# DeltaNet attention followed by a SwiGLU feed-forward block on one core: turning K and x with transfers and VectorE instead of TensorE

## The chip, the cores and the metric

The kernel runs on one core of a Trainium2 chip. The metric is the device time of one execution in microseconds (us), lower is better. A core has five engines with a queue of instructions each: TensorE (PE in the profile; its weight loads are the row PEld), VectorE (DVE), ScalarE (ACT), GpSimd (POOL) and SyncE (SP, which here only issues transfers). Sixteen DMA engines move the data of the transfers.

## The reference

There are 4 batches of 8 heads, 768 steps and a head dimension of 48. The result of the attention (`x`, 3072 tokens by 384) goes through a feed-forward block with 1536 inner columns. All is 32-bit floating point.

```python
k_n = k / (np.linalg.norm(k, axis=-1, keepdims=True) + 1e-06)
for t in range(S):
    kt, vt, bt = (k_n[:, :, t], v[:, :, t], beta[:, :, t, None])
    y[:, :, t] = np.einsum('bhd,bhde->bhe', q[:, :, t], state)
    v_old = np.einsum('bhde,bhd->bhe', state, kt)
    state = state + bt[:, :, :, None] * np.einsum('bhd,bhe->bhde', kt, vt - v_old)
x = y.transpose(0, 2, 1, 3).reshape(B * S, H * D)
rms = np.sqrt(np.mean(x * x, axis=-1, keepdims=True) + 1e-06)
xn = x / rms * rms_g
g = xn @ w_gate
out = (g * (1.0 / (1.0 + np.exp(-g))) * (xn @ w_val)) @ w_out
```

## The kernel before

The 768 steps are cut into 12 chunks of 64 steps, numbered c = 0 to 11; a chunk holds all 32 pairs of batch and head. Each chunk passes through these parts.

- `load` brings K, Q and V of the chunk into SBUF, with steps on the partitions. From chunk 2 on, Q comes as 16 small transfers that lay 32x32 squares into the tile `q2`, each square where its turned image belongs; in `qpart` one VectorE instruction (L592) then turns all squares of `q2` in place into `qt`, which has the head dimension on the partitions.
- `norms` and `prep` scale K to unit length (the power on GpSimd at L577, the product on GpSimd at L654), turn it (`turn`, L532 on TensorE into two PSUM banks, L544 on ScalarE out of them into `kt`), multiply it with itself (`scores`, L555), and invert a unit triangular matrix of each pair of batch and head. For the inversion the products go through DRAM (`dkk`) into the tile `at`, GpSimd scales them (L682), VectorE runs fifteen steps of multiply and reduce (L731, L737), and the result goes through DRAM again (`dx`, `dxt`) into `mt`, `x2bd` and `m1bd`; two small merges on TensorE follow (L813, L837).
- `recur` combines the chunk with the state carried from chunk to chunk (L878, L924, L938, L975). The chunk's output stands in `yn`, is normalised there (GpSimd for the root, ScalarE L1040 for the product) and turned on TensorE (L1046, six transposes of 128x128 in two PSUM banks) and scaled by `rms_g` on the way out of PSUM (L1055, six ScalarE instructions) into `xf`, which has the model dimension on the partitions. Seven VectorE sums of columns of `xf` follow (L1070).
- The feed-forward part of chunks 0 and 1 is plain (`ffn_plain`, L1118 and L1100). From chunk 2 on, `ffn` multiplies 3x3 blocks with 15 products instead of 18 for each half of the inner columns (L1211), with factors that VectorE computes once from the weights (`factors`, L1174 and L1176). The partial sums leave PSUM through VectorE (L1221) or ScalarE (L1223), then silu (L1227) and the product (L1228) fill `hf`; `down` makes the output with seven products of 2x2 blocks (L1268) and VectorE sums around them (L1260, L1277).

Single buffers set much of the order: `xf`, `yn`, `q2`, `qt`, `at` and `acc` exist once, `kt` twice, K three times. The next chunk's x can enter `xf` only when the last L1211 product of the chunk before has read it.

The order of instructions is made ahead by a planner in the kernel file (`Plan`). Each step is put in with its engine, an assumed duration, a due time, what it reads and writes, and the PSUM banks it needs. `forward` simulates the queues with those assumed durations, `backward` turns the result into new priorities, 110 rounds are played with small random shakes, and the best order is emitted. The order of each engine's queue is fixed then, and an instruction that waits holds up all that stands behind it on its engine. Transfers are nearly all issued by SP (L407). `turn` is the part of TensorE's work that the change takes away for most chunks:

```python
P.add("PE", 0.44, tr, pr, r=r + ["ident"], w=[ps, keys[hv]], ps=ps, size=8)
```

Of the kernel before, what the change touches and what calls it, by code (L numbers as in the profile page):

```python
# [11 lines left out]
FP32 = mybir.dt.float32  # L12
# [7 lines left out]
W = 32  # L20
# [9 lines left out]
RING, LANES, FIRST, LAND = 2330, 8, 1.08, 0.9  # L30
WARM = 62.0
CLEAR = (0.5, 0.8, 1.1)


class Op:
# [31 lines left out]
class Plan:  # L67
# [47 lines left out]
    def forward(self, banks, until, clear=1.0):  # L115

        at = dict.fromkeys(ENGINES, 0.0)
        held = {"DVE": 0.0, "POOL": 0.0}
        cand = {e: [] for e in ENGINES}
        free = list(banks)  # L120
        for op in self.ops:
            op.wait, op.at = len(op.deps), op.ready
            for g in op.acquire:
                g.taken, g.uses = False, g.left
            if not op.wait:
                cand[op.eng].append(op)
        order, end_, mode = [], 0.0, 0
        server, sent = 0.0, []
        landed = [0.0] * LANES
        soon = sorted((op.past, op.n) for op in self.ops if op.dma and not op.bulk and op.past is not None)  # L130
        backlog = 0.0
        while len(order) < len(self.ops):
            best = None
            for e in ENGINES:
                for op in cand[e]:
                    s = max(op.at, at[e])
                    if op.dma:
                        s = max(s, landed[-LANES])
                        if op.bulk:
                            for t, _ in soon:  # L140
                                if t >= max(server, s + FIRST) + clear * op.work:
                                    break
                                if t > s:
                                    s = t + 0.01
                    if op.port:
                        s = max(s, held["POOL" if e == "DVE" else "DVE"])
                    n = sum(not g.taken for g in op.acquire)
                    if n > len(free):
                        continue
                    if n:  # L150
                        s = max(s, free[n - 1])
                    key = op.key + (STICK if op.mode is not None and op.mode != mode else 0.0)
                    rate, store = (FETCH, AHEAD) if s > EARLY else (FETCH0, AHEAD0)
                    if op.size and backlog + op.size - rate * op.dur > store:
                        key += 2.0 * STICK
                    if best is None or (s, key, op.n) < best[0]:
                        best = ((s, key, op.n), op)
            if best is None:
                return None
            (s, _, _), op = best  # L160
            cand[op.eng].remove(op)
            for g in op.acquire:
                if not g.taken:
                    g.taken = True
                    free.pop(0)
            op.start = s
            if op.mode is not None and op.mode != mode:
                s += 0.1
                op.start, mode = s, op.mode
            end = s + op.dur  # L170
            if op.eng == "PE":
                if s - at["PE"] > 1.4 and s > until:
                    end += 1.6
                rate, store = (FETCH, AHEAD) if s > EARLY else (FETCH0, AHEAD0)
                fill = 6.0 if s < until else 0.0
                backlog = max(0.0, backlog - (rate - fill) * (s - at["PE"])) + op.size - rate * op.dur
                late = max(0.0, backlog - store) / rate
                backlog, end = max(0.0, backlog - rate * late), end + late
            at[op.eng] = end - min(OVERLAP[op.eng], op.dur)
            if op.port:  # L180
                held[op.eng] = end
            end_ = max(end_, end)
            for g in op.release:
                g.uses -= 1
                if not g.uses:
                    free.append(end + 0.1)
                    free.sort()
            if op.dma:
                end = self.room(sent, end, op.desc)
                at[op.eng] = end  # L190
                begun = max(server, s + FIRST)
                server = max(begun + op.work, end)
                if not op.bulk and op.past is not None:
                    soon.remove((op.past, op.n))
                sent.append((begun, server, op.desc))
                end = server + LAND
                landed.append(end)
            op.end = end
            for u in op.users:
                u.wait -= 1  # L200
                u.at = max(u.at, at[op.eng] if u.eng == op.eng and not op.dma else end + op.hop(u) + u.slack)
                if not u.wait:
                    cand[u.eng].append(u)
            order.append(op)
        self.end = end_
        return order
# [78 lines left out]
def kernel(  # L285
# [17 lines left out]
    nc = tc.nc  # L303

    B, H, S, D = q.shape
    NCH = S // C
    DM = H * D
    DFF = moe_w_gate.shape[1]
    KT = DM // 128
# [22 lines left out]
    g_sb = sbt("g_sb", [128, KT])  # L332
# [12 lines left out]
    q2 = sbt("q2", [128, 16, DP])  # L345
# [48 lines left out]
    banks = [psum.tile([128, 512], FP32, name=f"bank{i}") for i in range(8)]  # L394
    dkk = [dram.tile([2, 2, 16, W, W], FP32, name=f"dkk{i}") for i in range(2)]
    dx = [dram.tile([2, 2, 16, W, W], FP32, name=f"dx{i}") for i in range(2)]
    dxt = [dram.tile([W, 2, 16, W], FP32, name=f"dxt{i}") for i in range(2)]

    P = Plan()
# [5 lines left out]
    def dma(dst, src, prio, r=(), w=(), work=0.2, dur=0.53, eng="SP", after=0.0, desc=256, bulk=False):  # L405
        queue = nc.scalar if eng == "ACT" else nc.sync
        op = P.add(eng, dur, lambda: queue.dma_start(out=dst, in_=src), prio, r, w, lat=0.1)  # L407
        op.dma, op.work, op.ready, op.desc, op.bulk = True, work, after, desc, bulk
        op.port = False
# [136 lines left out]
    def scores(kt_, rhs, pr, r, w):  # L546

        ps = [Group(), Group()]

        def sc():  # L550
            for u in range(8):
                for d in range(2):
                    for g in range(2):
                        s, c_ = slice(64 * d, 64 * d + 64), slice(64 * g, 64 * g + 64)
                        nc.tensor.matmul(ps[d].t[c_, 64 * u : 64 * u + 64], kt_[s, u, c_], rhs[s, u, c_])  # L555

        P.rows = 64
        P.add("PE", 0.99, sc, pr, r=r, w=ps + w, ps=ps, size=128)
        P.rows = 128
        return ps  # L560
# [42 lines left out]
    def prep(c):  # L603
# [50 lines left out]
        P.add(n_, 1.6 if c else 1.1, lambda: en.tensor_tensor(  # L654
            out=kd, in0=kd, in1=krec[i2][:, :, None].to_broadcast([128, 16, D]), op=ALU.mult,
        ), pr if early else pn, r=[("krec", i2)], w=kkeys)
        turn(kn, kt[ikq], ktk, kkeys + kp, pr, False)
        ps = scores(kt[ikq], kt[ikq], pr, ktk, kkall)
        for d in range(2):
            dst = kk[ikk][:, :, d:16:2]  # L660
# [195 lines left out]
    def recur(c):  # L856
# [137 lines left out]
        for h in halves:  # L994
# [35 lines left out]
            if c == 0:  # L1030
                for g in range(2):
                    for p in h:
                        P.add("ACT", A(192), lambda p=p, g=g: nc.scalar.activation(
                            out=yn[:, p].rearrange("s (y g e) -> s y g e", g=2, e=D)[:, :, g],
                            in_=psy[g, p].t[:, 192 * p : 192 * p + 192].rearrange("s (y e) -> s y e", e=D),
                            func=ACTF.Copy, scale=rs[i2][:, p : p + 1],
                        ), py, r=[psy[g, p], ("rs", i2, p)], w=[("yn", p)], last=psy[g, p])
            else:
                for p in range(2):
                    P.add("ACT", A(384), lambda p=p: nc.scalar.mul(yn[:, p], yn[:, p], rs[i2][:, p : p + 1]), py, r=[("rs", i2, p)], w=[("yn", p)])  # L1040
            for p in h:
                psx = Group()

# [63 lines left out]
    def ffn_plain(c, f0, f1, start):  # L1107
# [19 lines left out]

        def down(f):
            if f == f0:
                P.add("PE", 0.0, lambda: None, start, r=xk, w=["po"], ps=po[1])  # L1130
            P.add("PE", 1.31, down_mm(po, f, f0, f1), start + 3.9 * (f - f0) + 9, r=[("hf", f, 0), ("hf", f, 1), "wouse"] + ready[("wo", f)], w=["po"], ps=po[0], size=8)

        LAG = 2
# [64 lines left out]
    def ffn(c, start):  # L1198
        n = 0
        for h in range(2):  # L1200
            ps = [Group() for _ in range(3)]
            for m, ((kind, slot), xs, b_, begin, o, more_, end) in enumerate(PRODUCTS):
# [11 lines left out]
                            )  # L1214

                first = ["acq"] if m < 3 else []
                P.add("PE", 0.9, mm, start + 0.95 * n, r=["xc", ("xp", 0), ("xp", 1), ("wx", h)], w=[g] + first, ps=g, size=16)
                n += 1
                t = tmp[:, o]
                if more_:  # L1220
# [108 lines left out]
    for c in range(NCH):  # L1329
# [13 lines left out]
        if c + 1 < NCH:  # L1343
            P.late = c > 0
            load(c + 1, "v")
            P.slack = 0.2
            qpart(c + 1)
            P.late = True
        if c + 2 < NCH:
            load(c + 2, "q")  # L1350
        P.slack, P.lead, P.late = 0.1, 0.0, c > 1
        if c == 1:

# [50 lines left out]
```

## Time and profile before

| | |
|---|---|
| median of 3 runs | 702.61 us (699.99 to 702.84) |
| the profiled execution | 702.7 us, with a span of 700.9 us from first to last instruction |
| granted TensorE clock | 1.000 |
| busy: PE, PEld | 685.0 us, 624.4 us |
| busy: DVE, ACT, POOL | 529.2 us, 311.6 us, 135.4 us |
| transfers | 54.66 MB in 232790 packets |

The profile is of one execution. Busy times are sums over an engine's instructions. Matmuls are pipelined: the duration of one is longer than the distance to the next, so distances between starts in the timeline tell what a group costs. L numbers are lines of the kernel before; 1.8 us of the profiled execution lie outside its span.

### The profile page before, as it was taken

What the parts mean: (1) busy time and instruction counts of PE and PEld (TensorE: products, weight loads), DVE (VectorE), ACT (ScalarE), POOL (GpSimd) and SP (SyncE); (2) the same over time, 40 slices, a digit from 0 to 9 for tenths busy, and PEclk for the clock granted to TensorE, in tenths of its full rate; (3) what the DMA queues carried; (4) which work ended last, traced back from release to release, by engine and by line L of the source; (5) the groups of instructions that cost most, each with busy time, mean ns of one, the idle gap of its engine ahead of it and who ended that gap; (6) DMA issues with size and microseconds to landing.
All of it is one profiled execution on the core that took longest, in us unless ns stands there. A gap on an engine that the chain in (4) does not pass through costs nothing.

```text
span 700.9 us, 23147 instructions
## 1 busy us (share of the span) xinstructions
PE 685.0 (98%) x9930; PEld 624.4 (89%) x9930; DVE 529.2 (76%) x1121; ACT 311.6 (44%) x720; POOL 135.4 (19%) x140
## 2 busy tenths in 40 slices
PE   9999799999999999999999999999999999999997
PEld 5667677787799999999999999999999999999997
DVE  4897794589889679639948969859947968957373
ACT  5256375552244445445344445345345345235241
POOL 6100040111123212132123132122105031000000
PEclk9999999999999999999999999999999999999999
DMA  7875894951623433251073261264153060130101
GB/s 115 154 173 107 196 268 71 273 103 24 119 49 48 82 64 46 43 105 26 21 122 52 39 130 26 40 105 71 35 80 57 13 121 15 24 56 2 23 1 23
DMA packets 232790, 54.66 MB, mean 78 GB/s; under 512 B 221936, under 2 KB 225008, under 8 KB 232688
## 3 DMA queue, kind: packets, MB, share of 16 engines
q1 hardware_dynamic: 227840, 52.27, 39.6%
q10 hardware_dynamic: 4848, 0.92, 0.8%
q8 instruction: 78, 1.28, 0.8%
q14 instruction: 24, 0.20, 0.1%
HBM read 40.83 MB, written 12.32 MB: 76 GB/s over the span
## 4 chain that ended last, share of the span: by engine, by line
PE 73%; DVE 14%; DMA 5%; SPq 3%; POOL 2%; issue 2%; ACT 2%; DVEq 0%; POOLq 0%; ACTq 0%
PE bank L1211 32%; PE bank L1268 18%; PE bank L1118 5%; PE bank L1100 3%; PE bank L555 3%; SPq L407 3%; PE bank L878 2%; PE bank L1368 2%; DMA more<-in_moe_w_gate_dram 2%; DVE tmp L1221 2%; DVE acc L737 2%; DVE acc L731 2%; PE bank L532 2%; PE bank L924 1%; PE bank L837 1%
## 5 line engine op out<-in xcount | busy, mean ns | idle before, releaser
L1211 PE MATMUL bank<-xf,w_in 128*128 128x128 f32 x1440 | 181.0, 277 | 0.0
L1221 DVE TENSOR_TENSOR tmp<-tmp,bank 128x512 f32<-128x512 f32 x180 | 120.9, 683 | 74.6 <-PE bank L1211 57.1
L1211 PEld LDWEIGHTS bank<-xf,w_in 128*128 128x128 f32 x1440 | 170.5, 192 | 3.0 <-issue 1.2
L1211 PE MATMUL bank<-xf,more 128*128 128x128 f32 x960 | 124.6, 277 | 2.1 <-DVE tmp L1221 2.1
L1211 PEld LDWEIGHTS bank<-xf,more 128*128 128x128 f32 x960 | 115.3, 192 | 4.2 <-DVE tmp L1221 3.2
L1223 ACT COPY tmp<-bank 128x512 f32<-128x512 f32 x120 | 68.8, 585 | 92.2 <-PE bank L1211 62.9
L737 DVE TENSOR_REDUCE acc<-acc 128x30 f32<-128x90 f32 (+4 forms) x180 | 85.1, 473 | 6.2
L1227 ACT ACTIVATE tmp<-tmp 128x256 f32<-128x256 f32 x120 | 49.5, 417 | 86.7 <-DVE tmp L1221 86.2
L1268 PE MATMUL bank<-wo_sb,hf 128*128 128x192 f32 x360 | 64.3, 328 | 0.0
L577 POOL TENSOR_TENSOR knrm<-ksum,half 128x16 f32<-128x16 f32 x12 | 36.0, 3003 | 145.7 <-DVE ksum L576 145.7
L731 DVE TENSOR_TENSOR acc<-acc,at 128x60 f32<-128x60 f32 (+4 forms) x165 | 59.1, 358 | 6.6 <-POOL at L714 4.4
L1268 PEld LDWEIGHTS bank<-wo_sb,hf 128*128 128x128 f32 x360 | 58.1, 190 | 0.5
L1228 DVE TENSOR_TENSOR hf<-tmp 128x256 f32<-128x256 f32 x120 | 49.8, 431 | 11.0 <-ACT tmp L1227 10.4
L1368 PE MATMUL bank<-ident 128*128 128x128 f32 (+2 forms) x154 | 45.3, 440 | 1.4 <-POOL ident masks.py:199 1.4
L758 POOL COPY acc<-acc 128x128 f32<-128x128 f32 x40 | 18.1, 480 | 131.9 <-DVE acc L737 131.0
L1368 PEld LDWEIGHTS bank<-ident 128*128 128x128 f32 x154 | 26.2, 197 | 18.4 <-issue 15.7
L1118 PE MATMUL bank<-xf,w_in 128*128 128x256 f32 x144 | 34.9, 386 | 4.1 <-DVE w_in L496 3.7
L682 POOL TENSOR_TENSOR at<-at,beta_b 128x1024 f32<-128x1024 f32 x8 | 18.8, 2356 | 93.4 <-DMA at<-dkk 75.9
L1118 PEld LDWEIGHTS bank<-xf,w_in 128*128 128x128 f32 x144 | 26.4, 190 | 10.4 <-DVE w_in L496 4.5
L1100 PE MATMUL bank<-wo_sb,hf 128*128 128x384 f32 x96 | 33.6, 488 | 0.0
L1118 PE MATMUL bank<-xp,w_in 128*128 128x256 f32 x144 | 33.1, 382 | 0.4 <-DVE hf L1126 0.4
L1118 PEld LDWEIGHTS bank<-xp,w_in 128*128 128x128 f32 x144 | 27.0, 190 | 5.4 <-DVE hf L1126 0.5
(166 smaller groups left out, 980.9 us busy)
## 6 DMA issues: line engine op xcount, KB each, us to landing
at<-dkk SPq DMA_DIRECT2D x21, 256.0 KB, 4.1
vt<-in_v_dram SPq DMA_DIRECT2D x24, 192.0 KB, 4.1
more<-in_moe_w_gate_dram SPq DMA_DIRECT2D x6, 768.0 KB, 7.7
more<-in_moe_w_val_dram SPq DMA_DIRECT2D x6, 768.0 KB, 8.4
more<-in_moe_w_out_dram SPq DMA_DIRECT2D x6, 768.0 KB, 5.8
out_dram<-tmp SPq DMA_DIRECT2D x48, 96.0 KB, 2.3
k<-in_k_dram SPq DMA_DIRECT2D x23, 192.0 KB, 4.1
mt<-dx SPq DMA_DIRECT2D x84, 32.0 KB, 2.0
```

Of the source, the lines that this page charges most:

```text
L577: P.add("POOL", 2.95, lambda: nc.gpsimd.tensor_tensor(out=knrm[i2], in0=ksum[i2], in1=half, op=ALU.pow), pn, r=[("ksum", i2), "half"], w=[ ...
L731: nc.vector.tensor_tensor(out=acc[:, 1:3, 0:n, j + 2 : W].rearrange("p a i t -> p i a t"), in0=acc[:, old, 0:n, j : j + 2, None].to_broadc ...
L737: nc.vector.tensor_reduce(out=acc[:, new, 0:n, j + 2 : W], in_=acc[:, lo : lo + 3, 0:n, j + 2 : W].rearrange("p a i t -> p i t a"), axis=A ...
L1100: nc.tensor.matmul(po[p].t[:, 0:DM], hf[:, spot(f), 128 * p : 128 * p + 128], wo_sb[:, spot(f)], start=(f == f0), stop=(f == f1 - 1), skip ...
L1118: nc.tensor.matmul(ps.t[:, TOK * side : TOK * side + TOK], w_in[:, side, h_, 3 * t + i_, n : n + 128], x_[:, 2 * t : 2 * t + 2].rearrange( ...
L1211: nc.tensor.matmul(g.t[:, 128 * z : 128 * z + 128], fac[:, side, 128 * f : 128 * f + 128], xf[:, xs], start=(begin and z == 0), stop=False ...
L1221: P.add("DVE", V(512), lambda t=t, g=g: nc.vector.tensor_tensor(out=t, in0=t, in1=g.t, op=ALU.add), -1, r=[g], w=[tk], last=g)
L1223: P.add("ACT", A(512), lambda t=t, g=g: nc.scalar.copy(t, g.t), -1, r=[g], w=[tk], last=g)
L1227: P.add("ACT", A(256), lambda t=t: nc.scalar.activation(out=t[:, 0:256], in_=t[:, 0:256], func=ACTF.Silu), -1, w=[tk])
L1228: P.add("DVE", V(256), lambda t=t, f0=f0, p=p: nc.vector.tensor_tensor(out=hf[:, spot(f0) : spot(f0) + 2, 128 * p : 128 * p + 128], in0=t[ ...
L1268: nc.tensor.matmul(g.t[:, 0:192], a_[:, f], b_[:, f], start=(begin and f == 0), stop=(f == 5), skip_group_check=True)
L1368: nc.tensor.matmul(warm[:, 0 : 128 * w_].rearrange("p (w n) -> p w n", n=128), ident, ident[:, None, :].to_broadcast([128, w_, 128]))
```

## The change

For chunks 3 to 11, K is turned in the way that Q already was. After its scaling, sixteen transfers from SBUF to SBUF lay its 32x32 squares into `q2`, which K and Q now use by turns, and one VectorE instruction turns them into `kt`. For chunks 2 to 10, x takes such a way too: four transfers write the normalised `yn` to a DRAM buffer `xd`, four bring it back into `yn` as squares, two VectorE instructions turn it into `xf`, and three ScalarE instructions multiply `xf` by `rms_g` in place. The K of chunks 0 to 2 and the x of chunks 0, 1 and 11 stay on TensorE.

Three smaller edits go with it. The products of K and Q read 48 instead of 64 rows, because the squares leave the rows behind the head dimension unset. The loading of Q is put in ahead of `qpart` of the same chunk, behind the K that shares its buffer. The first three products of each `ffn` wait until the last `ffn_plain` has begun its down products (`begun`). The edits in `forward` skip candidates that can't win and leave its choice the same. The planner works out a new order for the whole kernel.

```diff
+TURNK = range(3, 12)
+TURNX = range(2, 11)
...
+    xd = [dram.tile([4, 128, 6, W], FP32, name=f"xd{i}") for i in range(2)]
...
-                        s, c_ = slice(64 * d, 64 * d + 64), slice(64 * g, 64 * g + 64)
+                        s, c_ = slice(64 * d, 64 * d + D), slice(64 * g, 64 * g + 64)
...
-        turn(kn, kt[ikq], ktk, kkeys + kp, pr, False)
+        if c in TURNK:
+            for d, eh, g, th in itertools.product(range(2), repeat=4):
+                e0, e1 = 32 * eh, min(D, 32 * eh + 32)
+                r0, s0 = 64 * d + 32 * eh, 64 * g + 32 * th
+                dma(q2t[r0 : r0 + 32, :, g, th, 0 : e1 - e0], kn[s0 : s0 + 32, d:16:2, e0:e1], pr, r=kkeys, w=[q2k[8 * d + 4 * eh + 2 * g + th]], work=0.21)
+            P.add("DVE", V(1024), lambda: nc.vector.transpose(out=kt[ikq].rearrange("p u t -> p (u t)"), in_=q2.rearrange("p x e -> p (x e)")), pr, r=q2k + ["q2p"], w=ktk)
+        else:
+            turn(kn, kt[ikq], ktk, kkeys + kp, pr, False)
...
+            if c in TURNX:
+                blocks = yn.rearrange("s p (t j e) -> s (p t) j e", t=KT, j=4)
+                flat = yn.rearrange("s p n -> s (p n)")
+                for j in range(4):
+                    dma(xd[i2][j], blocks[:, :, j], py, r=[("yn", 0), ("yn", 1)], w=[("xw", j)], work=0.7, desc=768)
+                for j in range(4):
+                    dma(flat[W * j : W * j + W].rearrange("s (i n) -> s i n", i=4), xd[i2][j].rearrange("(i r) a e -> r i (a e)", i=4), py, r=[("xw", k_) for k_ in range(4)], w=[("yl", j)], work=0.2, desc=128)
+                squares = flat.rearrange("s (i p t e) -> s p i t e", i=4, p=2, t=KT)
+                for p in range(2):
+                    P.add("DVE", V(384), lambda p=p: nc.vector.transpose(
+                        out=xdst[:, p:6:2].rearrange("s t (i e) -> s i t e", i=4), in_=squares[:, p]
+                    ), pxv, r=[("yl", j) for j in range(4)], w=[("yn", 0), ("yn", 1), xkeys[p]])
+                for t in range(KT):
+                    P.add("ACT", A(256), lambda t=t: nc.scalar.mul(xdst[:, 2 * t : 2 * t + 2], xdst[:, 2 * t : 2 * t + 2], g_sb[:, t : t + 1]), pxv, r=["g"], w=xkeys)
+                continue
...
-                P.add("PE", 0.0, lambda: None, start, r=xk, w=["po"], ps=po[1])
+                P.add("PE", 0.0, lambda: None, start, r=xk, w=["po", "begun"], ps=po[1])
...
+                plain = ["begun"] if m < 3 else []
...
+            if c:
+                P.late = True
+                load(c + 1, "q")
             P.slack = 0.2
+            P.late = c > 0
             qpart(c + 1)
             P.late = True
-        if c + 2 < NCH:
-            load(c + 2, "q")
```

More of the change, by code (lines that the diff above doesn't have):

```diff
@@ L132, in forward @@
         while len(order) < len(self.ops):
-            best = None
+            best, soonest = None, 1e9
             for e in ENGINES:
+                free_at = at[e]
+                if free_at > soonest:
+                    continue
                 for op in cand[e]:
-                    s = max(op.at, at[e])
+                    s = op.at if op.at > free_at else free_at
+                    if s > soonest:
+                        continue
                     if op.dma:
@@ L156, in forward @@
                     if best is None or (s, key, op.n) < best[0]:
-                        best = ((s, key, op.n), op)
+                        best, soonest = ((s, key, op.n), op), s
             if best is None:
@@ L1040, in recur @@
                     P.add("ACT", A(384), lambda p=p: nc.scalar.mul(yn[:, p], yn[:, p], rs[i2][:, p : p + 1]), py, r=[("rs", i2, p)], w=[("yn", p)])
+            if c in TURNX:
[12 more added lines that the diff above has]
+                    P.add("ACT", A(256), lambda t=t: nc.scalar.mul(xdst[:, 2 * t : 2 * t + 2], xdst[:, 2 * t : 2 * t + 2], g_sb[:, t : t + 1]), pxv, r=["g"], w=xkeys)
+                continue
             for p in h:
@@ L1216, in ffn @@
                 first = ["acq"] if m < 3 else []
-                P.add("PE", 0.9, mm, start + 0.95 * n, r=["xc", ("xp", 0), ("xp", 1), ("wx", h)], w=[g] + first, ps=g, size=16)
+                plain = ["begun"] if m < 3 else []
+                P.add("PE", 0.9, mm, start + 0.95 * n, r=["xc", ("xp", 0), ("xp", 1), ("wx", h)] + plain, w=[g] + first, ps=g, size=16)
                 n += 1
```

## The prediction

> **What bounds the kernel now.** I read the page first: the busy rows, then the slices.
>
> ```profile
> PE 685.0 (98%) x9930; PEld 624.4 (89%) x9930; DVE 529.2 (76%) x1121; ACT 311.6 (44%) x720; POOL 135.4 (19%) x140
> ...
> PE   9999799999999999999999999999999999999997
> ...
> DVE  4897794589889679639948969859947968957373
> ...
> PEclk9999999999999999999999999999999999999999
> ```
>
> TensorE is busy from end to end at the full granted clock (1.000), VectorE is next. A busy PE may still stand still in ways that a sum hides, so I looked at the table by stage (us; then busy and count of PE, PEld, DVE, ACT, POOL; clock; DMA share; GB/s) and at PE's own waits in each stage.
>
> ```profile
> 156.00:227.00 71.00, 69.93 (x877) 60.30 (x875) 64.10 (x124) 24.62 (x59) 14.29 (x13) 1.00 0.35 59
> 279.00:330.00 51.00, 49.79 (x820) 48.02 (x819) 33.25 (x76) 22.87 (x57) 12.68 (x13) 1.00 0.36 64
> 381.00:432.00 51.00, 51.00 (x830) 49.60 (x829) 43.22 (x94) 23.92 (x58) 12.32 (x14) 1.00 0.37 64
> 535.00:588.00 53.00, 53.00 (x802) 51.37 (x794) 44.42 (x99) 24.68 (x60) 16.43 (x18) 1.00 0.28 50
> ```
>
> In the steady part a chunk takes some 52 us, all of it PE. Between 381 and 432 the list of PE's waits is empty; between 279 and 330 it holds one wait of 1.2 us on the VectorE sum L1221. The chunk's time is therefore PE's issue time, and what leaves PE's queue leaves the clock, as long as nothing new makes PE wait. Two stages have less room: 156 to 227, where VectorE works 64.1 of 71 us (weight conversion, factors, inversion), and the end, which the change does not touch.
>
> The timeline shows what the turns cost (start, duration of the group, what):
>
> ```profile
> 224.91 1.04 PE L532 MATMUL bank<-ident,k 128*128 128x128 f32 x8
> 225.78 1.06 PE L1211 MATMUL bank<-xf,w_in 128*128 128x128 f32 x8
> 226.68 0.91 PE L1046 MATMUL bank<-ident,yn 128*128 128x128 f32 x6
> ```
>
> Not the 1.04 us counts, nor the 273 ns of one transpose, since matmuls overlap: the next group starts 0.87 us later, 0.109 us for each of the eight transposes.
>
> **What is removed.** Nine K turns of 8 transposes. Their start-to-start cost is 0.87 us in three of them that I looked at (at 147.1, 224.9, 289.6) and 0.93 at 546.9: 9 x 0.87 = 7.8 us. Nine x turns of 6 transposes: 0.74 us at 226.7, 0.81 at 280.8, 0.75 at 333.1 and 543.8, so 9 x 0.76 = 6.9 us. The order of the changed kernel has exactly 72 and 54 transposes less on PE, and all products are still there. Together **14.7 us** leave PE's queue. ScalarE loses 18 copies of 0.587 us and 54 of 0.369 us and gains 27 products of 128x256, 0.417 us each by L1227: 30.5 us out, 11.3 in; it is under half busy, so I count nothing.
>
> The row says that no wait was left in a steady chunk. [...]
>
> **What is added on VectorE.** Nine instructions like L592, and eighteen of 128x384.
>
> ```profile
> L592 DVE STREAM_TRANSPOSE qt<-q x10: 1233/1238/1245, 97.7 to 567.8; 128x1024 f32<-128x1024 f32 x10
> ```
>
> 9 x 1.24 = 11.1 us; a 128x384 turn scaled by elements is 0.46 us, 18 x 0.46 = 8.4 us. Per chunk 2.2 us on an engine that works 33 to 44 of some 51 us there; it becomes 46.6 of about 50 in the fullest. VectorE has gaps of 10 us in a chunk (for one, it waits for L1211 results from 510 to 535), but it also has stretches of 30 us without a gap, at the start of a chunk's products, where the x turns will stand. There a late L1221 or L1277 keeps a PSUM bank from PE. Between 279 and 381 PE has three such waits (1.2, 0.8 and 0.3 us, 2.3 in all). Bounds: a re-planned order may lose these (-2.3 us), or each of nine chunks may wait the whole 2.2 us (+19.8). I take +1.5 us, nearer to the lower end, because in 381 to 535 VectorE works up to 43.2 us of a chunk without one PE wait.
>
> Between 148 and 190 us VectorE runs without a gap, and there two of the new turns land: x of chunk 2 (0.93 us) and, by the order of the changed kernel, K of chunk 4 (1.24), which stood at 225 before. PE waited for VectorE 0.4 and 0.2 us there already. Bounds 0 and 2.2 us; I take **+1.2**, about half, since the first L1211 product that needs the factors starts 12 us after the last factor of its half.
>
> **What is added on SP and the DMA engines.** 24 transfers per chunk. An issue takes 0.5 us (nine Q issues in 4.53 us), so SP gets 12 us more on the 44 issues, 22 us, that a chunk has: 34 of 50.
>
> ```profile
> q1 hardware_dynamic: 227840, 52.27, 39.6%
> ...
> mt<-dx SPq DMA_DIRECT2D x84, 32.0 KB, 2.0
> q<-in_q_dram SPq DMA_DIRECT2D x80, 32.0 KB, 2.8
> ...
> dx<-acc SPq DMA_DIRECT2D x20, 128.0 KB, 3.1
> ```
>
> These lines of the page are a queue's packets, MB and share, and transfers with their size and microseconds to landing. A chunk gets 4096 packets for K and 3584 for x. The queue's row gives 0.396 x 16 x 700.9 / 227840 = 0.0195 us for a packet, so 7680 packets are 150 us spread over 16 engines, 9.4 us a chunk: the DMA share goes from 0.37 to about 0.55. No bound there; the price can only lie in latency.
>
> *K's latency* (16 issues, 8 us, and 2.8 to land, then 1.24) is some 12 us in place of 2. What is late next is `dkk`, `at` and the inversion, but GpSimd stands idle 24.1 us for `at` up to 532.7, and the result of an inversion is needed a period later. Nothing.
>
> *x's latency.* From the end of L938 (534.45) until `yn` is normalised (540.96) are 6.5 us. Then four issues 2.0, landing 3.1 by the `dx` row, four issues 2.0, landing 2.0 by the `mt` row: 9.1. Then two turns 0.9, three ScalarE products 1.25, seven sums L1070 2.6: 4.8. Together 20.4 us until the next chunk's products can begin. The order of the changed kernel puts between L938 and those products, at the shortest, L975 (0.83), 32 matmuls of old products (7.15 at 0.2235), two scores (2.18), a state product (1.08) and six down products (11.7): 22.9 us, in other chunks up to 26. The slack is 2.5 to 5.6 us, about 4; I count nothing.
>
> **The sum**, against the profiled execution's 702.7 us (0.1 over the median): 702.7 - 14.7 + 1.5 + 1.2 = 690.7, say **690.5 us**. With no loss and the old waits gone it is 685.7; with 4 us more lost, 695.
>
> **Rivals.** *VectorE becomes the bound* (15%). For: 64 of 71 us at 156 to 227, and 30 us without a gap in each chunk. Against: gaps of 10 us a chunk. If 2.2 us is lost in the early stage and 0.9 us in each of eight chunks, 702.7 - 14.7 + 9.4 = 697.4.
>
> *The x trip is late, slower* (13%). SP works in order, and in the changed kernel K's sixteen issues stand right ahead of the four that write `xd`, chunk after chunk. K's issues wait for GpSimd's scaling and for `q2`, which Q must have left. If they go out only when `yn` is ready, x starts 8.0 us later, 4.0 over its slack, and PE has nothing of the next chunk: 9 x 4.0 = 36, so 702.7 - 14.7 + 2.7 + 36 = 726.7 us. It decides at 12.0 / 9 = 1.33 us late per chunk, a trip of 14.4 us in place of 9.1. For: the single `q2` serves K and Q now, and `yn` stays taken longer. Against: Q's squares go the same way already and nobody waited for L592. The Trainium skill ("DMA: Bandwidth & Descriptors", Rules for kernel authors) speaks for this rival: transfers under 64 KB pay mostly overhead and should be merged, and K's are 32 and 16 KB; no run shows yet what they cost on x's path.
>
> *Little is left* (8%): both losses in part, 12 of 14.7 us, near 700. That the change leaves the turns on PE can't be, by the order.
>
> **How the numbers follow.** My forecast has 64%, with its own range 685.5 to 695; VectorE 15%, 695 to 699; little left 8%, to 706; slower 13%. A measurement of this kernel can tell 0.5%, 3.5 us, from no change: faster is 0.79, same 0.08, slower 0.13. The range 685.5 to 703 leaves out the slow case and some of the third.
>
> **What would show it.** PE should have 126 instructions less of both kinds and a span shorter by about 12 us; the distance between the L924 groups of following chunks (52.7 us from 424.8 to 477.5) should fall by 1.4 to 1.6; the new turns should take 1.24 and 0.46 us. I am wrong if PE waits at the first product of a chunk for the sums of `xf`, or if SP's waits ahead of the `xd` transfers are longer than the slack; VectorE as the bound would show as PE waits on L1221 spread over each chunk.

## The result: 6.7% slower

The changed kernel takes 749.79 us (median of 4 runs, 747.99 to 751.40) against 702.73 us for the kernel before (4 runs): a ratio of 1.0666, 95% interval 1.0636 to 1.0696. The forecast was 690.5 us with a range up to 703, so both size and sign are wrong. Times are medians of all executions, while the ratios leave out executions more than 1.5% above the fastest of their kernel (four of ten with K in five issues, one and three of ten in the two runs with x alone), so a ratio is not quite the quotient of the times beside it. The profiled execution took 751.4 us with a span of 749.7. L numbers from here on are those of the kernel shown, and differ by a few lines between the runs; in the changed kernel the old L924 is L939, L1211 is L1241, L1221 is L1252, L1268 is L1299.

The page of the changed kernel, first its busy rows and clock, then the chain that ended last:

```profile
PE 695.3 (93%) x9796; PEld 626.6 (84%) x9796; DVE 562.7 (75%) x1148; ACT 298.9 (40%) x675; POOL 137.3 (18%) x140
...
PEclk9988999999899999999899899999999999999999
...
PE 45%; SPq 22%; DVE 13%; DMA 11%; issue 5%; ACT 3%; POOL 2%; DVEq 0%; POOLq 0%; ACTq 0%
SPq L415 22%; PE bank L1241 21%; PE bank L1299 11%; DVE acc L752 3%; DVE tmp L1252 2%; PE bank L1130 2%; PE bank L939 2%; PE bank L1148 2%; DVE acc L746 2%; PE bank L1401 2%; DMA dx<-wsum 1%; DVE xf L1100 1%; PE bank L852 1%; DMA at<-dkk 1%; DMA out_dram<-tmp 1%
```

The transposes have left PE, yet PE is busy 10 us longer, and idle 54.4 us instead of 15.9. The chain of the kernel before reads:

```profile
PE 73%; DVE 14%; DMA 5%; SPq 3%; POOL 2%; issue 2%; ACT 2%; DVEq 0%; POOLq 0%; ACTq 0%
```

SP's queue (SPq) had 3% there and PE 73%. Now the single line that issues transfers, L415, is the first entry.

The table by stage shows where (us; busy and count of PE, PEld, DVE, ACT, POOL; granted clock; DMA share; GB/s). The rows of the changed kernel:

```profile
381.00:432.00 51.00, 46.50 (x791) 44.57 (x789) 41.57 (x81) 19.43 (x47) 10.71 (x10) 0.94 0.50 82
227.00:641.00 414.00, 383.79 (x5932) 367.64 (x5931) 332.04 (x679) 165.16 (x385) 88.52 (x90) 0.98 0.46 76
```

Between 381 and 432 PE was busy all 51.00 us before; now 46.50, at a clock of 0.94. The distance between the L939 groups of following chunks is 58 to 62 us in the steady part, in place of 52.7. The DMA engines are half free on average, DVE works 332 of the 414 us and ACT 165: no sum of busy time explains this.

The SP queue's own timeline does (start, duration of the group, what; `xN` is the number of issues). First a place of the kernel before, with Q's sixteen squares; behind the next K the queue issues nothing for 10 us:

```profile
431.52 0.66 SPq L407 DMA_DIRECT2D k<-in_k_dram  x1
432.28 8.91 SPq L407 DMA_DIRECT2D q<-in_q_dram  x16
441.29 0.60 SPq L407 DMA_DIRECT2D k<-in_k_dram  x1
451.89 1.16 SPq L407 DMA_DIRECT2D out_dram<-tmp  x2
```

In the changed kernel, one chunk:

```profile
459.28 11.39 SPq L415 DMA_DIRECT2D q<-k  x16
470.78 1.40 SPq L415 DMA_DIRECT2D k<-in_k_dram  x2
472.28 0.68 SPq L415 DMA_DIRECT2D dxt<-acc  x1
473.06 4.03 SPq L415 DMA_DIRECT2D xd<-yn  x4
477.14 0.65 SPq L415 DMA_DIRECT2D dxt<-acc  x1
477.83 1.34 SPq L415 DMA_DIRECT2D dx<-acc  x2
479.26 2.28 SPq L415 DMA_DIRECT2D q<-in_q_dram  x2
481.65 0.39 SPq L415 DMA_DIRECT2D yn<-xd  x1
482.08 2.06 SPq L415 DMA_DIRECT2D dkk<-kk  x4
484.19 1.46 SPq L415 DMA_DIRECT2D yn<-xd  x3
```

There is hardly a gap: each issue begins where the one before ends, within 0.11 us. SP is not waiting for data here; it is at work issuing. K's sixteen take 11.39 us, and only then come the raw K, `dxt`, and x's four `xd` transfers, though `yn` was normalised at 469.8. The last `yn<-xd` is out at 485.65. The other engines in the same place:

```profile
468.60 1.16 ACT L1055 ACTIVATE yn<-yn,rs 128x384 f32<-128x384 f32 x2
487.77 1.04 DVE L1065 STREAM_TRANSPOSE xf<-yn 128x384 f32<-128x384 f32 x2 [5.46 <-DMA m1bd<-dxt]
488.85 1.31 ACT L1069 ACTIVATE xf<-xf,g_sb 128x256 f32<-128x256 f32 x3 [5.27 <-DVE xf L1065]
490.06 0.29 ACT L1304 COPY tmp<-bank 128x192 f32<-128x192 f32 x1
490.41 3.90 PE L1299 MATMUL bank<-wo_sb,xp 128*128 128x192 f32 x12 [3.29 <-ACT tmp L1304]
```

The turn starts 18.0 us after `yn` was ready. Of these 3.3 pass before the first `xd` goes out (0.9 behind K's squares, the rest behind the raw K and `dxt`), 4.0 in issuing `xd`, 4.6 until the first `yn<-xd`, 4.0 until the last is out, and 2.1 until the turn. DVE stood idle for 5.46 us ahead of it (the profile names the transfer `m1bd<-dxt` as what ended that, but L1065 reads `yn` alone, and `m1bd<-dxt` was issued right behind the last `yn<-xd`). ACT's product waited 5.27 us, the copy L1304, which has nothing to do with x, stood behind that product in ACT's queue, and PE waited for the copy. When PE went on, its group took 3.90 us instead of 2.11.

The transfers themselves don't land later: from issue to landing `xd<-yn` takes 2.9 us in the median between 227 and 641 (4.1 in this chunk), and 2.8 where x alone is turned this way. Most of the time is lost ahead of the issues and in them.

The waits of PE over the whole execution (us in total, times, longest) look harmless one by one:

```profile
PE bank L1299 <- ACT tmp L1304: 10.0, 3, 4.5
PE bank L563 <- DVE kt L670: 8.4, 7, 3.5
```

The first holds the one just followed, the second is K itself: PE's products of K wait for its turn. A list of waits by PE alone names ACT and DVE and not the cause.

### The profile page after: what moved, and what is told of

Same layout as the page of the kernel before. It is cut to its first block, busy times and chain, and to the rows that moved or that the text cites. A ratio compares the mean times of both kernels' runs of the same rounds, so it can differ in the third digit from the quotient of the medians.

```text
span 749.7 us, 23184 instructions
## 1 busy us (share of the span) xinstructions
PE 695.3 (93%) x9796; PEld 626.6 (84%) x9796; DVE 562.7 (75%) x1148; ACT 298.9 (40%) x675; POOL 137.3 (18%) x140
## 2 busy tenths in 40 slices
DMA packets 305368, 65.30 MB, mean 87 GB/s; under 512 B 289904, under 2 KB 297584, under 8 KB 305264
## 4 chain that ended last, share of the span: by engine, by line
PE 45%; SPq 22%; DVE 13%; DMA 11%; issue 5%; ACT 3%; POOL 2%; DVEq 0%; POOLq 0%; ACTq 0%
SPq L415 22%; PE bank L1241 21%; PE bank L1299 11%; DVE acc L752 3%; DVE tmp L1252 2%; PE bank L1130 2%; PE bank L939 2%; PE bank L1148 2%; DVE acc L746 2%; PE bank L1401 2%; DMA dx<-wsum 1%; DVE xf L1100 1%; PE bank L852 1%; DMA at<-dkk 1%; DMA out_dram<-tmp 1%
## 5 line engine op out<-in xcount | busy, mean ns | idle before, releaser
L1241 PE MATMUL bank<-xf,w_in 128*128 128x128 f32 x1440 | 182.3, 279 | 1.4 <-DVE tmp L1252 1.2
L1241 PEld LDWEIGHTS bank<-xf,w_in 128*128 128x128 f32 x1440 | 171.1, 193 | 5.0 <-DVE tmp L1252 1.7
L1252 DVE TENSOR_TENSOR tmp<-tmp,bank 128x512 f32<-128x512 f32 x180 | 119.7, 679 | 49.9 <-PE bank L1241 38.6
L1241 PE MATMUL bank<-xf,more 128*128 128x128 f32 x960 | 126.0, 279 | 1.0 <-DVE tmp L1252 0.7
L1241 PEld LDWEIGHTS bank<-xf,more 128*128 128x128 f32 x960 | 116.0, 193 | 4.0 <-DVE tmp L1252 1.9
L1258 ACT ACTIVATE tmp<-tmp 128x256 f32<-128x256 f32 x120 | 49.9, 417 | 116.1 <-DVE tmp L1252 115.9
L752 DVE TENSOR_REDUCE acc<-acc 128x30 f32<-128x90 f32 (+4 forms) x180 | 85.0, 472 | 6.2
L1299 PE MATMUL bank<-wo_sb,hf 128*128 128x192 f32 x360 | 67.1, 339 | 8.5 <-ACT tmp L1304 6.8
L1299 PEld LDWEIGHTS bank<-wo_sb,hf 128*128 128x128 f32 x360 | 60.6, 196 | 10.1 <-ACT tmp L1304 7.3
L746 DVE TENSOR_TENSOR acc<-acc,at 128x60 f32<-128x60 f32 (+4 forms) x165 | 56.9, 345 | 10.1 <-POOL at L729 7.7
L1100 DVE TENSOR_TENSOR xf<-xf 128x256 f32<-128x256 f32 (+1 forms) x70 | 41.9, 633 | 5.4 <-ACT xf L1069 4.6
L1130 PE MATMUL bank<-wo_sb,hf 128*128 128x384 f32 x96 | 37.1, 527 | 0.0
L1148 PEld LDWEIGHTS bank<-xf,w_in 128*128 128x128 f32 x144 | 28.2, 201 | 6.0 <-issue 1.1
L1299 PE MATMUL bank<-wo_sb,xp 128*128 128x192 f32 x120 | 24.2, 357 | 9.4 <-DVE xp L1291 6.1
```

The costliest lines, as they stand in the source:

```text
L746: nc.vector.tensor_tensor(out=acc[:, 1:3, 0:n, j + 2 : W].rearrange("p a i t -> p i a t"), in0=acc[:, old, 0:n, j : j + 2, None].to_broadc ...
L752: nc.vector.tensor_reduce(out=acc[:, new, 0:n, j + 2 : W], in_=acc[:, lo : lo + 3, 0:n, j + 2 : W].rearrange("p a i t -> p i t a"), axis=A ...
L1130: nc.tensor.matmul(po[p].t[:, 0:DM], hf[:, spot(f), 128 * p : 128 * p + 128], wo_sb[:, spot(f)], start=(f == f0), stop=(f == f1 - 1), skip ...
L1148: nc.tensor.matmul(ps.t[:, TOK * side : TOK * side + TOK], w_in[:, side, h_, 3 * t + i_, n : n + 128], x_[:, 2 * t : 2 * t + 2].rearrange( ...
L1241: nc.tensor.matmul(g.t[:, 128 * z : 128 * z + 128], fac[:, side, 128 * f : 128 * f + 128], xf[:, xs], start=(begin and z == 0), stop=False ...
L1252: P.add("DVE", V(512), lambda t=t, g=g: nc.vector.tensor_tensor(out=t, in0=t, in1=g.t, op=ALU.add), -1, r=[g], w=[tk], last=g)
```

## The experiments

In what was expected, A is x's trip standing late behind K's issues, B (later called S) that K's sixteen issues by themselves hold up SP's queue, C the new order and the small edits, Q the shared `q2`, D the packets, L the latency of K's own trip. Each kernel was timed beside the kernel before on the same chip; ratios are to it, with 95% intervals. "Over neither" is the difference of a ratio to that of the third run, times 702.7 us.

**K alone, x alone, neither.** The parts of the change were taken out by the ranges of chunks; the rest of the change stays.

```diff
-TURNX = range(2, 11)
+TURNX = range(0)      # K alone
-TURNK = range(3, 12)
+TURNK = range(0)      # x alone; both edits: neither
```

> Only K of chunks 3 to 11 goes through squares; x stays on TensorE. Theory A (x comes late because its eight transfers stand behind K's sixteen on SP): without x there is nobody to be late, PE loses nine turns of 0.87 us and little else, 692 to 706 us. Theory B (K's sixteen issues of 0.65 us and the shared q2 hold up SP's whole queue, whoever stands behind): 725 us or more. Theory C (the new order made by the planner costs by itself, from the prologue on): above 715 us.

> Only x of chunks 2 to 10 goes through DRAM and squares; K stays on TensorE. Theory A: without K's issues ahead of it the trip of x falls from 18 us to about 10 to 13, inside its cover, so 700 to 715 us. Theory B: near 700. Rival (the trip of x is too long by itself): 730 us or more, with PE still waiting at the first products of a chunk.

> The smaller edits alone (Q loaded ahead of its qpart, 48 rows in the scores, the begun key), K and x on TensorE as before. Theory A and B: 698 to 708 us, as before. Theory C (the re-plan or the smaller edits cost): 715 us or more, with the first chunk's L953 some 5 us late as in the changed kernel.

Measured: K alone 724.74 us, 1.0297 (1.0277 to 1.0317); x alone 701.80, 0.9979 (0.9953 to 1.0005); neither 697.59, 0.9915 (0.9888 to 0.9943). The new order and the small edits are no loss but a gain of about 6 us, so C falls. K alone was to stay under 706 by A and to reach 725 by B; it is at B's edge, so A alone is not enough. x alone fits both. Over neither, K alone costs 27 us, x alone 4.5, both together 53: some 21 us are lost only where both are in. The page's PE row and chain of the run with neither show the old state:

```profile
PE 685.3 (99%) x9924; PEld 623.9 (90%) x9924; DVE 535.6 (77%) x1121; ACT 312.7 (45%) x720; POOL 145.8 (21%) x140
...
PE 81%; DVE 5%; SPq 4%; DMA 4%; POOL 2%; issue 1%; ACT 1%; ACTq 0%; POOLq 0%; DVEq 0%
```

**True costs for the planner.** The planner takes an issue for 0.53 us. In the changed kernel the trace says (duration ns min/median/max, first and last start):

```profile
L415 SPq DMA_DIRECT2D q<-in_q_dram x164: 312/449/2212, 15.5 to 619.4; - x164
L415 SPq DMA_DIRECT2D q<-k x144: 595/609/1949, 102.7 to 586.9; - x144
L415 SPq DMA_DIRECT2D xd<-yn x36: 554/660/2190, 154.8 to 642.7; - x36
L415 SPq DMA_DIRECT2D yn<-xd x36: 315/441/2023, 175.8 to 646.8; - x36
```

Q's squares and K's have the same shapes, but out of DRAM an issue takes 0.45 us and out of SBUF 0.61; from start to start K's are 0.655 us apart. The whole change was planned anew with 0.66 and 0.67:

```diff
-... w=[q2k[8 * d + 4 * eh + 2 * g + th]], work=0.21)
+... w=[q2k[8 * d + 4 * eh + 2 * g + th]], work=0.21, dur=0.66)
-dma(xd[i2][j], blocks[:, :, j], ..., work=0.7, desc=768)
+dma(xd[i2][j], blocks[:, :, j], ..., work=0.7, desc=768, dur=0.67)
```

> The whole change, but the planner is told 0.66 us for an issue of a K square and 0.67 for one of xd, as the trace has them, in place of 0.53. If the loss is that the planner believed x in time (theory A with wrong costs as its cause), the order moves and the time falls to 715 to 735 us; if x can't be in time with this much on one queue, or the costs don't matter, 742 to 757 us.

Measured: 729.14 us, 1.0374 (1.0327 to 1.0420). 20.5 us come back, about two fifths of the 53; the transfers are the same, only their places differ.

**K's issues on ACT's queue** (K alone).

```diff
-dma(q2t[...], kn[...], ..., work=0.21)
+dma(q2t[...], kn[...], ..., work=0.21, dur=0.65, eng="ACT")
```

> K alone (x on TensorE), its sixteen issues put on ScalarE's queue and costed at 0.65 us each; buffer, packets and turn stay as in e1_k_only. Theory S (SP's issue time for K's squares, 0.65 us where 0.53 was planned, holds up all that stands behind on SP): SP is free again, 700 to 712 us. Theory Q (the shared q2 makes K and Q wait for each other) or D (the packets themselves): 718 to 730 us, as e1_k_only. ScalarE gets 10 us more per chunk; if that is what counts, waits on its PSUM copies appear and the time is above 715.

Measured: 722.91 us, 1.0294 (1.0262 to 1.0325), as much as on SP; the 700 to 712 that B (S) asked for was missed. SP is issuing no more than in the kernel before (table below), but an issue is as long on ACT, and ACT has work of its own behind it (issues; then ACT's waits):

```profile
L415 ACTq DMA_DIRECT2D q<-k x144: 592/621/1943, 99.2 to 552.4; - x144
```

```profile
ACT tmp L1254 <- DMA q<-k: 19.0, 5, 5.7
ACT tmp L1258 <- DMA q<-k: 10.2, 3, 7.1
```

These copies empty PSUM for PE; they stand behind issues in ACT's queue. That these 29 us are what keeps the time up is likely and not shown. The Trainium skill ("DMA: Bandwidth & Descriptors", Rules for kernel authors) says that spreading transfers over issuing engines saves only the issuing sequencer's time. Here SP's issuing fell from 467 to 347 us, and the time of the kernel did not change.

**K's squares without `q2`** (K alone: they go straight into `kt`, which is turned in place; `q2` is Q's again).

```diff
-dma(q2t[r0 : r0 + 32, :, g, th, 0 : e1 - e0], kn[...], ...)
+dma(ktt[r0 : r0 + 32, :, g, th, 0 : e1 - e0], kn[...], ...)
-nc.vector.transpose(out=kt[ikq]..., in_=q2...)
+nc.vector.transpose(out=kt[ikq]..., in_=kt[ikq]...)
```

> K alone, but its squares are laid into kt itself and turned there in place, so q2 serves Q alone; the issues stay on SP at the planned 0.53 us. Theory Q: 698 to 710 us. Theory S: 716 to 728 us, the lag of SP behind its plan growing by some 2 to 3 us a chunk as in e1_k_only.

Measured: 730.23 us, 1.0415 (1.0370 to 1.0461), no better than with the shared buffer and a little above the 716 to 728 of S. Q, with 698 to 710, falls.

**K's squares read from DRAM** (the whole change; SP, PE, DVE and ACT have the same order of instructions as in the changed kernel; the squares come from the K input and are not scaled, nor do they wait for the scaling).

```diff
-dma(q2t[...], kn[s0 : s0 + 32, d:16:2, e0:e1], ...)
+dma(q2t[...], k.rearrange("b (yh a) t e -> a t (b yh) e", a=4)[2 * d + g, c * C + 32 * th : c * C + 32 * th + 32, :, e0:e1], ...)
```

> The whole change in the same planned order, but K's squares are read from K in DRAM, so K is turned without its scaling (the output is not the reference's) and the transfers no longer wait for GpSimd's product. An issue should fall from 0.65 to 0.50 us as for Q. Theory S: 16 x 0.15 = 2.4 us a chunk and the waits on L662 go, and what follows from them: 715 to 735 us. If neither issue time nor that wait is the cost: 743 to 755 us.

Measured: 725.91 us, 1.0314 (1.0257 to 1.0372): 25 us less than the changed kernel, with as many transfers and as many packets (305,368 on both pages). What changed in the queue is the length of an issue:

```profile
L415 SPq DMA_DIRECT2D q<-in_k_dram x144: 311/449/2108, 101.4 to 565.7; - x144
```

16 x 0.16 us is 2.6 us a chunk, 23 us in nine chunks. The missing wait for the scaling may have a part in it too.

**x alone with true costs** (0.67 for the `xd` issues, 0.5 for the ScalarE products).

```diff
-dma(xd[i2][j], blocks[:, :, j], ..., work=0.7, desc=768)
+dma(xd[i2][j], blocks[:, :, j], ..., work=0.7, desc=768, dur=0.67)
-P.add("ACT", A(256), ... xdst ...)
+P.add("ACT", 0.5, ... xdst ...)
```

> x alone, with the planner told 0.67 us for an issue of xd and 0.5 us for each ScalarE product, as measured. If the 4 us that e2_x_only lost against e3_neither come from those costs: 690 to 698 us, under e3_neither's 697.6 by up to the 6.9 us of TensorE. If the trip itself costs: 699 to 705 us.

Measured: 704.42 us, 1.0012 (0.9977 to 1.0047). This is what was set down for the case that the trip itself costs. x by itself gains nothing from a better plan and ends near the kernel before.

**Sixteen issues that nobody needs.** The run with neither, and in chunks 3 to 11 sixteen transfers of K's squares on SP to a DRAM buffer that nothing reads.

```diff
+if c >= 3:
+    for d, eh, g, th in itertools.product(range(2), repeat=4):
+        ...
+        dma(kdr[c % 2][8 * d + 4 * eh + 2 * g + th, :, :, 0 : e1 - e0], kn[s0 : s0 + 32, d:16:2, e0:e1], pr, r=kkeys, w=[...], work=0.21)
 turn(kn, kt[ikq], ktk, kkeys + kp, pr, False)
```

> Neither K nor x is turned through transfers (both on TensorE, as in the run with neither, 697.6 us); the only addition is that sixteen transfers a chunk with the shape of K's squares go on SP's queue at the same place, to a DRAM buffer that nothing reads, planned at 0.53 us each. Theory S (the issue time itself holds up SP's in-order queue, and Q, x and the raw inputs behind it): sixteen issues of 0.6 to 0.66 us are some 10 us of SP a chunk although no engine waits for what they carry, so most of the 27 us by which K alone lost should come back: 712 to 725. Rival L (the cost is K's own round trip, the wait of PE and DVE for the squares): nobody waits here, so 696 to 703.

Measured: 737.39 us, 1.0485 (1.0433 to 1.0538), 40 us over neither and above both expectations. Nothing of the mechanism of the change is left in this kernel, no turn, no latency, no shared buffer; the issues alone cost more than K's whole detour. L falls as the cause of the whole. What stands behind them comes later: from the last copy of the products into `kk` until the four `dkk` issues are out it takes 6.3 us in the median of eight chunks, against 2.7 in the run with neither, and until GpSimd takes up `at` 14.4 against 11.7. GpSimd's wait for `at` grows from 92.2 to 146.3 us, for a transfer that was there before and shares the queue; only 5.7 us, once, are put down to the idle transfers. PE meets it further on: its largest wait, 13.0 us in five times, is for the sums on VectorE that empty its banks (L1258), and just ahead of all five VectorE runs steps of the inversion (L752, L758), which begins at `at`.

**The same, planned with 0.66 us for each idle issue.**

```diff
-w=[...], work=0.21)
+w=[...], work=0.21, dur=0.66)
```

> The run with the sixteen idle issues (737.4 us), but the planner is told 0.66 us for each of them instead of 0.53; nothing else changes, and nobody waits for what they carry. Of the 40 us by which that run was slower than the one with neither: if the planner's too small number does the harm (it puts Q, the raw inputs and the small transfers behind a queue that it takes to be free sooner), most of it comes back, 698 to 715. If the sixteen issues do the harm by the time that they hold the in-order queue, whatever the planner knows, little comes back: 722 to 737. About half, as in the whole change (20.7 us of 52): 715 to 722, both.

Measured: 722.65 us, 1.0232 (1.0174 to 1.0290), 22 us over neither. Both reasons, at the border of what was set down for the second: 18 of the 40 us go with the planner's wrong number, 22 stay although it knows the right one. In this run SP has 6% of the chain and VectorE 20%, against 4% and 5% in the run with neither: most of what stays shows at VectorE, and how the issues, or the order that makes room for them, come to that was not taken apart.

**Five issues instead of sixteen** (K alone: one write of K to DRAM, four reads of the squares from there; then the same with x as in the change).

```diff
+dma(kdr[i2], kn, pr, r=kkeys + kp, w=[("kw", i2)], work=1.0, desc=128)
+for d, eh in itertools.product(range(2), repeat=2):
+    ...
+    dma(q2s[r0 : r0 + 32, :, :, 0 : e1 - e0], kdr[i2].rearrange("(a r) x e -> r x a e", r=32)[:, d:16:2, :, e0:e1], pr, r=[("kw", i2)], w=q2k[n0 : n0 + 4], work=0.84, dur=0.66, desc=1024)
```

> K alone, through transfers, but in 5 issues a chunk instead of sixteen: one write of K (128 x 1024) to DRAM and four reads of 1,024 packets each. The squares that DVE turns are the same; the trip gets a landing longer (two in a row, some 2 us each and more). Theory S (sixteen issues on SP): 11 issues a chunk fewer, 7 us of SP, so at most a few us over the run with neither: 690 to 704. Rival L (K's round trip): the trip is no shorter, so 715 to 730. Rival D (the packets themselves: here there are three times as many): 725 to 745.

> The whole change with K in the 5 issues of the run before, x as in the change. Theory S: x's eight issues no longer stand behind sixteen, so x costs what it cost alone (some 4 us over neither): 692 to 708. If x's own trip is late whatever K does (rival A alone): 715 to 735. If the packets count (rival D): over 735.

Measured: K alone 706.77 us, 1.0013 (0.9974 to 1.0052), 7 us over neither instead of 27 (10 by the quotients of the medians), at the upper end of S's range. With x 721.04 us, 1.0244 (1.0187 to 1.0302), 30 us less than the changed kernel, but not in S's range: it lies in A's. With eleven issues fewer ahead of it x's trip is 14.2 us in the median, between 11.8 alone and 18.0 in the changed kernel, so x is less late and still late. It is not K's issues that it then stands behind: the first `xd` goes out within 1.8 us of the normalised `yn` in every chunk. In two chunks (trips of 23.8 and 20.9 us) VectorE works without a gap and takes the squares late; in one of them they had landed 12.1 us before. The chain of this run has VectorE with 26% and SP with 8%. The premise on packets in the expectation was wrong: the write goes in whole rows, and the page counts hardly a packet less or more than for K alone in sixteen issues (271,961) or for the idle ones (271,960):

```profile
DMA packets 271527, 62.92 MB, mean 89 GB/s; under 512 B 259520, under 2 KB 262592, under 8 KB 271424
```

So D falls: with as many packets and more bytes, eleven issues a chunk fewer cost 20 us less than K alone, and 33 less than the idle issues. Its plan knew the issues' length, though; against the idle issues at true cost it is 15 us. The premise on K's trip was wrong as well: it is shorter, 10.3 us from GpSimd's product to the turn in the median of nine chunks, against 14.5 in K alone. Against K alone, then, this run doesn't part L from S. Against the idle issues it does, for these have no trip at all and cost more. The issues:

```profile
L417 SPq DMA_DIRECT2D q<-kdr x36: 568/676/1608, 103.2 to 542.7; - x36
L417 SPq DMA_DIRECT2D kdr<-k x9: 345/351/1248, 97.7 to 535.7; - x9
```

Together, with the time for which SP's queue is issuing in the profiled execution (durations of its issues added up over the whole span, with gaps under 0.1 us between issues of the same kind):

| kernel | SP issuing, us | ratio |
|---|---|---|
| neither | 335 | 0.9915 |
| before | 344 | 1 |
| K alone, issues on ACT | 347 | 1.0294 |
| x alone | 387 | 0.9979 |
| K in five issues | 390 | 1.0013 |
| K in five issues, x | 428 | 1.0244 |
| sixteen idle issues | 444 | 1.0485 |
| K alone, squares in `kt` | 456 | 1.0415 |
| sixteen idle issues, true cost | 459 | 1.0232 |
| K alone | 467 | 1.0297 |
| whole change, K from DRAM | 482 | 1.0314 |
| the changed kernel | 508 | 1.0666 |
| whole change, true costs | 510 | 1.0374 |

Where SP issues for up to some 390 us the time stays within 1% of the kernel before, but for the run that gave the issues to ACT; from 428 on every kernel loses some 2% or more. Inside that group the order is not that of the column; how well the plan knows the cost counts as well. Each row is one plan: how far another plan of the same kernel would lie from it was not measured, so differences of a few us between rows carry little. The only kernel that is clearly faster than the kernel before is the one with neither turn, 697.59 us.

## Why the prediction was wrong

- **Failed: "No bound there; the price can only lie in latency"** (the part on SP). The count of issues was right, 24 more a chunk; the duration was not. The 0.5 us came from Q's issues out of DRAM; K's out of SBUF are 0.655 apart, and the four `xd` issues took 4.03 us in the chunk shown. I wrote 34 of 50 us a chunk, 22 of them from before and 12 new. Over the seven chunks between 227 and 641 SP was issuing 322 of 414 us, 46 a chunk, against 26 before: 20 new. 46 of the 52.7 us that PE used to need leaves 6 for all waits of an in-order queue; what waited before is late now. The idle issues show it as a cause: 40 us, 22 with honest planning.
- **Failed: x's trip, "9.1" us with a slack of about 4.** From the normalised `yn` to the first turn it is 18.0 us in the median of nine chunks (9.9 to 27.8). x alone has 11.8, its first `xd` issue going out at once in every chunk; in the changed kernel it goes out 3.3 us late in the median (0 to 10.9). So about 2.7 us were a wrong sum and some 6 come with K's issues in the queue, ahead of `xd` and between its parts.
- **Failed: K's latency, "Nothing".** From the scaled K to its turn it is 14.1 us in the median of nine chunks, where 8 and 2.8 were foretold. DVE waits 21.8 us for K's squares in eight chunks, and PE 8.4 us for the turned K in seven. How large a part of the 27 us of K alone this is, is not shown; the idle issues, where it is absent, cost 40, and 22 with honest planning.
- **Right in mechanism, too cheap: the rival "The x trip is late, slower"**, with a chance of 13%. K's issues ended near the time when `yn` was ready, between 1.0 us before and 10.8 after in seven of nine chunks, the trip of 18.0 us passed the 14.4 from which it was to decide, and PE stood still. Its price, 726.7, let x start 8.0 us late (3.3 in the median) and charged x alone; but K's issues hold up all transfers, x or no x, and x's product stands in front of other copies in ACT's queue. A time of 749.79 us was in no rival.
- **Right: what leaves PE.** The transposes are off PE (9,796 records against 9,930; some records are missing from a trace). A gain can't be read off the total, as the lost clock covers it.
- **Right, nearly: VectorE.** K's turn takes 1.245 us (1.24 foretold), x's 0.574 (0.46). VectorE is no bound in the changed kernel: PE's waits for L1252 are 1.9 us in all. With K in five issues and x it comes nearer to one (26% of the chain).
- **The planner.** That its 0.53 us is too small for the new issues stood in the code and was seen by no step of mine. It is some 18 to 20 us of the loss by the two pairs of runs with and without true costs.

What stays open: with K in five issues, x still costs 16 us more, where x alone costs 4.5, though SP was issuing only 428 us. Its trip is 2.4 us longer there than alone, and the chain points to VectorE as much as to the queue; how that becomes 16 us was not taken apart. The same holds for the 22 us of the idle issues at true cost, and for the part that chance has in each plan.

## What to carry to other kernels

An engine that only issues transfers is an engine: add up its issues at the duration that the trace has for that source and destination, and hold the sum against the period of the loop, not against the bandwidth. Here eight transposes on the bound engine were replaced by sixteen small transfers in a queue that was issuing for half of the period already, and moving these to another in-order queue didn't help. When a planner makes the order, a wrong assumed cost of a new kind of step is an edit in itself; here it was worth about 20 us.

## What the runs showed of the hardware

The same square transfer takes 0.45 us to issue out of DRAM and 0.61 out of SBUF, on SP and on ACT (0.62) alike. The write of the same squares to DRAM takes 0.61 as well, a write of whole rows of K 0.35 in one run and 0.59 in the other (medians of nine), and a read of four squares' worth from DRAM, 1,024 packets, 0.68, so the source is not all; with four times the packets the read out of DRAM takes 0.23 us more. The Trainium skill ("DMA: Bandwidth & Descriptors", Anatomy of one DMA) counts some 50 ns for the sequencer's dispatch and a small part for the descriptors, in a passage on transfers issued from GpSimd. By that figure sixteen issues would be an estimated 0.8 us a chunk. The traces of this case, for transfers from SP and ACT, have 0.45 to 0.62 us for one issue, about ten times that, and 11.39 us for the sixteen in the chunk shown.

The wait on PE that was followed above cost twice. These are stages of the chunk shown (columns as above):

```profile
486.00:490.00 4.00, 1.12 (x7) 0.82 (x6) 1.88 (x3) 1.15 (x3) 0.00 (x0) 1.00 0.90 203
490.00:494.00 4.00, 3.59 (x12) 3.59 (x13) 3.75 (x6) 0.35 (x2) 2.27 (x1) 0.58 0.69 94
494.00:500.00 6.00, 5.87 (x84) 5.27 (x82) 4.65 (x10) 2.78 (x6) 3.84 (x5) 1.00 0.35 61
```

After 3.29 us without work the granted clock of the next 4 us is 0.58, and the L1299 group there took 3.90 us, not 2.11: 1.8 us more on top of the wait. Over the execution the clock is 0.97, which goes with PE's busy time having risen while its work fell: the 685.0 us of before, less 14.7 for the turns, over 0.97 are an estimated 691, and 695.3 were measured. The DMA engines, half free on average, were busy to 0.90 in the first of these stages.
